# A recurrence, a gated convolution and an FFT mixer on one core: the recurrence in 64-token halves and plain fp32

## The chip, the cores and the metric

The kernel runs on one core of a Trainium2 chip. TensorE multiplies matrices into PSUM (eight banks), VectorE, ScalarE and GpSimd work on tiles, and DMA queues move data; GpSimd works in SBUF alone. The metric is the time on the device in microseconds (us). One profiled execution was traced.

## The reference

Four batches, 768 tokens, eight heads of 40, width 320. Cut to what is computed:

```python
for t in range(S):                       # a recurrence with a state C of 40x40 and n of 40 per head
    m_new = np.maximum(f_gate[:, :, t] + m, i_gate[:, :, t])
    f_stab = np.exp(f_gate[:, :, t] + m - m_new)
    i_stab = np.exp(i_gate[:, :, t] - m_new)
    C = f_stab * C + i_stab * outer(vt, kt)
    n = f_stab * n + i_stab * kt
    y[:, :, t] = sigmoid(o_gate[:, :, t]) * (C @ qt) / np.maximum(np.abs(n @ qt), 1.0)
x = y.transpose(0, 2, 1, 3).reshape(B, S, 320)
gate = sigmoid(sum(conv_w[k] * xp[:, k:k + S, :] for k in range(5)))    # causal, by channel
x = (gate * (x @ w_val)) @ w_out
mixed = np.real(np.fft.fft(np.fft.fft(x, axis=1), axis=2))
u = x + mixed
un = (u - mean(u)) / np.sqrt(var(u) + 1e-06)
out = u + np.maximum(un @ w_ch1, 0.0) @ w_ch2                           # 320 -> 1280 -> 320
```

## The kernel before

Every operation is first recorded into a plan (`_Plan.add`, units of one engine each) and then issued in the order of a list, `ORDER`, written out for all engines at once; `CELL` names the buffer of each tile and `FILLS` says ahead of which unit how many filler matmuls (`fill`, L1099, tile `void`, 128 x 128 in fp32) go into TensorE's queue. All operations but the fillers carry line L332 in the profile, so they are told apart by their tiles.

A batch is worked in this order. The recurrence takes six chunks of 128 tokens (`loads`, `a_pre`, `a_s`, `a_p`, `a_u`, `a_pv`, `a_fin`, `a_tr`). The gates' decay is first made for all tokens (`prologue_gates`); per chunk, VectorE scans it into a 128 x 128 triangle per head (`d`, two scans of 512), from rows that a DMA spreads over 128 partitions (`scr`). Scores `s` are keys by queries: in batch 0 in plain fp32, with the heads of a pair in the lower and the upper 64 partitions; from batch 1 on in fp32r, for which q and k are split into a high and a low part (`a_split`, tile `HL`) and twelve DMAs a chunk set three copies one below the other (`qk3`, 120 rows). VectorE multiplies scores and decay. `u` is the chunk's update of the state (`kvo` by `kvo`, 40 columns), added into `cc` on GpSimd and VectorE and copied into a block-diagonal `cbd`; `pv` is the output from the state (`e` by `cbd`) and from the scores (`d` by `kvo`). `a_fin` divides and gates, `a_tr` transposes (`tp`) into halves of 384 tokens.

Per half, `p_conv` adds five shifted products (one on ScalarE, four on VectorE, tile `gate`), `p_val`, `p_g` and `p_z` multiply with `w_val` and `w_out` in fp32r, each operand split into high and low. `p_fold` (GpSimd) and `b_s`, `b_se`, `d_mm`, `b_d`, `b_de` do the two Fourier transforms by matmuls with cosine and sine tables (`ap`, `uv`), the tables and operands split as well. `b_ln` and `b_ut` normalise and transpose, and the MLP runs per 256 tokens in ten tiles of 128 hidden columns: `m_1` (`hp`, eight matmuls), ScalarE and VectorE split its relu into `hh` and `hl`, `m_2` adds six matmuls into two `acc`. Weights arrive as 64-bit numbers and are turned into fp32 on the chip (`to_f32`, tile `mk`, mostly VectorE). While one batch's MLP runs, the list works the next batch's recurrence in between.

Of the kernel before, what the change touches and what calls it, by code (L numbers as in the profile page):

```python
# [1236 lines left out]
```

## Time and profile before

| what | us |
|---|---|
| median of three runs (lowest, highest) | 582.0 (581.72, 584.56) |
| the profiled execution, its span | 583.1 |
| TensorE busy in it | 559.4 |
| VectorE busy | 428.3 |
| ScalarE, GpSimd busy | 250.8, 250.3 |

The span runs from the first to the last instruction of the profiled execution; the profile shows no time around it. A matmul counts as busy from its start to its modelled end, and fillers count as any matmul does, so TensorE's share says how full its queue is and not how much of the work is the kernel's own.

### The profile page before, as it was taken

Reading aid. Unit: us, or ns where it says so; the run is one execution under the profiler, and the core shown is the slowest. Engines: PE = TensorE matmul, PEld = TensorE weight load, DVE = VectorE, ACT = ScalarE, POOL = GpSimd, SP = SyncE. Lnnn points to the kernel's source line nnn. Section 1 sums busy time; section 2 is a strip of 40 time slices with the busy share of each in tenths; the row PEclk is TensorE's granted clock in tenths of the full one; section 3 lists DMA queues with packets and bytes.
Section 4 is the critical chain, followed back from the end, with each engine's and each line's share of the span. In section 5 each row is a group of like instructions: output and inputs, shape, how many; then the busy total and the mean of one; then the engine's idle time right before and its main releaser. Section 6 shows DMA issues by size and latency. Waiting matters only on the chain.

```text
span 583.1 us, 12342 instructions
## 1 busy us (share of the span) xinstructions
PE 559.4 (96%) x4564; PEld 542.7 (93%) x4564; DVE 428.3 (73%) x904; ACT 250.8 (43%) x635; POOL 250.3 (43%) x301
## 2 busy tenths in 40 slices
PE   9999999999999979899999999999999999999997
PEld 8999899989999869899899898899999999999997
DVE  6737989989788999976689867945997375484322
ACT  3322343443365444535355534454445353444221
POOL 5246567649656434547632313365441315220000
PEclk9999999999999987999899999999999999999999
DMA  9997453635546849445422756426541200000000
GB/s 289 273 248 188 145 125 99 174 113 163 177 148 185 258 143 239 147 146 163 139 70 73 219 177 197 103 69 194 148 143 50 76 2 22 1 2 24 24 24 22
DMA packets 90843, 75.83 MB, mean 130 GB/s; under 512 B 5536, under 2 KB 83488, under 8 KB 90784
## 3 DMA queue, kind: packets, MB, share of 16 engines
q1 hardware_dynamic: 90032, 72.80, 43.2%
q0 software_dynamic: 752, 2.25, 1.3%
q8 instruction: 36, 0.59, 0.4%
q14 instruction: 23, 0.19, 0.1%
HBM read 53.21 MB, written 4.13 MB: 98 GB/s over the span
## 4 chain that ended last, share of the span: by engine, by line
PE 59%; DVE 15%; DMA 12%; issue 5%; SPq 4%; ACT 2%; POOL 2%; DVEq 0%; POOLq 0%; ACTq 0%
PE acc L332 14%; PE hp L332 13%; PE void L1099 7%; PE pv L332 7%; DVE d L332 6%; PE ap L332 5%; SPq L332 4%; PE val L332 4%; PE zp L332 3%; DMA kvo<-in_kvo_dram 3%; PE tp L332 2%; DMA qk<-HL 2%; DMA raw<-in_w_dram 2%; DMA d<-scr 2%; DVE mk L332 2%
## 5 line engine op out<-in xcount | busy, mean ns | idle before, releaser
L1099 PE MATMUL void<-ones 128*128 128x128 f32 x866 | 106.6, 282 | 1.0 <-DVE mhalf L332 1.0
L1099 PEld LDWEIGHTS void<-ones 128*128 128x128 f32 x866 | 102.4, 197 | 1.7 <-DVE mhalf L332 1.0
L332 PE MATMUL hp<-uu,w1H 128*128 128x256 f32 x480 | 93.6, 287 | 2.7 <-DVE hl L332 1.3
L332 DVE SCALAR_TENSOR_TENSOR hl<-hp,hh 128x256 fp32r<-128x256 f32 x120 | 48.9, 415 | 46.0 <-ACT hh L332 44.5
L332 PEld LDWEIGHTS hp<-uu,w1H 128*128 128x128 f32 x480 | 75.9, 191 | 4.4 <-DVE hl L332 1.9
L332 PE MATMUL acc<-w2H,hl 128*128 128x320 f32 x240 | 77.0, 321 | 2.3 <-DVE hl L332 2.2
L332 PE MATMUL acc<-w2H,hh 128*128 128x320 f32 x240 | 78.2, 326 | 0.5 <-ACT hh L332 0.5
L332 ACT ACTIVATE hh<-hp 128x256 fp32r<-128x256 f32 x120 | 45.3, 379 | 72.9 <-PE acc L332 48.0
L332 PE MATMUL acc<-w2L,hh 128*128 128x320 f32 x240 | 75.5, 315 | 0.0
L332 DVE TENSOR_TENSOR_SCAN d<-d,ipat 128x512 f32<-128x512 f32 x44 | 67.5, 1563 | 1.9 <-DMA d<-scr 1.8
L332 PE MATMUL hp<-uu,w1L 128*128 128x256 f32 x240 | 67.8, 283 | 0.0
L332 DVE SCALAR_TENSOR_TENSOR gate<-xT,cw,gate 128x384 f32<-128x384 f32 x96 | 63.9, 693 | 5.1 <-ACT gate L332 4.9
L332 PE MATMUL pv<-kvo,d 128*128 128x41 f32 x384 | 54.4, 275 | 1.5 <-DVE d L332 1.3
L332 PEld LDWEIGHTS pv<-kvo,d 128*128 128x128 f32 x384 | 50.2, 193 | 2.3 <-DVE d L332 1.9
L332 PEld LDWEIGHTS acc<-w2H,hl 128*128 128x128 f32 x240 | 46.3, 193 | 5.1 <-DVE hl L332 4.6
L332 PEld LDWEIGHTS acc<-w2H,hh 128*128 128x128 f32 x240 | 46.4, 193 | 1.1 <-ACT hh L332 0.8
L332 PEld LDWEIGHTS acc<-w2L,hh 128*128 128x128 f32 x240 | 46.3, 193 | 0.0
L332 PEld LDWEIGHTS hp<-uu,w1L 128*128 128x128 f32 x240 | 45.9, 191 | 0.0
L332 POOL TENSOR_TENSOR kvo<-kvo,r 128x320 f32<-128x320 f32 x24 | 20.2, 843 | 50.6 <-DVE r L332 48.5
L332 POOL TENSOR_TENSOR e<-e,qk 128x512 f32<-128x512 f32 x20 | 27.6, 1383 | 26.1 <-issue 12.4
L332 DVE TENSOR_TENSOR d<-s,d 128x512 f32<-128x512 f32 x48 | 32.3, 679 | 6.2 <-POOL kvo L332 4.4
L332 PE MATMUL hp<-uu,w1T 128*128 128x256 f32 x120 | 33.9, 282 | 0.0
(171 smaller groups left out, 1260.9 us busy)
## 6 DMA issues: line engine op xcount, KB each, us to landing
qk<-HL SPq DMA_DIRECT2D x216, 80.0 KB
qk<-in_qk_dram SPq DMA_DIRECT2D x24, 512.0 KB
kvo<-in_kvo_dram SPq DMA_DIRECT2D x24, 484.0 KB
d<-scr SPq DMA_DIRECT2D x22, 512.0 KB
raw<-in_w_dram SPq DMA_DIRECT2D x9, 640.0 KB
e<-sce SPq DMA_DIRECT2D x40, 128.0 KB
out_dram<-z SPq DMA_DIRECT2D x24, 160.0 KB
cs<-in_c_cs_dram POOLq DMA_DIRECT2D x2, 776.0 KB, 6.2
```

What stands on the lines that cost most here:

```text
L332: getattr(engine, method)(*a, **k)
L1099: nc.tensor.matmul(out=void[0], lhsT=ones.real(), rhs=ones.real(), start=True, stop=True)
```

## The change

The recurrence works each chunk in two halves of 64 tokens: the decay triangles are 64 x 64 (`d` is 8 heads x 64, one scan), the scores, the update and the outputs are matmuls in plain fp32 on 64 partitions to 64 columns, and the state is carried twice a chunk (`cc` of three tiles; no `cbd`). The halves of odd heads are swapped on the host side. The split of q and k and its copies (`a_split`) are gone. The decay rows reach PSUM by a matmul with a selector (`a_fb`, `sel`, `gsp`) and no longer by DMA, and the scan reads them there. The convolution accumulates in PSUM, and five of its 24 pieces, all of batch 0, are matmuls with diagonal matrices (`diagonals`). The Fourier tables and operands are no longer split. The MLP's tiles are worked in pairs of 128 hidden columns. Some steps change engine (`XL`, `ES` to VectorE, the small steps of the norm, `N_`, to GpSimd), weight tails of 64 rows are converted two at a time and copied to the other 64 partitions by DMA, PSUM is one tile of eight banks that the list `CELL` hands out, `ORDER` is another list of 2,002 units (2,795 before), and the fillers named in `FILLS` are 75 (433 before).

```diff
+LS = 64
-BF = 1
-CF = 6
-LAG = 1
+NQK = 2
+PECONV = [(0, 0, 0), (0, 0, 1), (0, 0, 2), (0, 1, 0), (0, 1, 2)]
...
+FILLS = [
+    (137, 11, 5), (60, 2, 2), (64, 4, 6), (142, 6, 5), (165, 3, 6), (170, 4, 2), (226, 6, 6), (390, 1, 1), (396, 7,
+    4), (401, 2, 2), (435, 2, 1), (459, 4, 1), (464, 2, 1), (488, 13, 6), (518, 8, 6),
+]
...
+                if k.pop("drain", False):
+                    engine.drain()
...
+    def fill(n, k):
+        a = pat.real()[:, 0:L]
+        for _ in range(n):
+            nc.tensor.matmul(out=banks()[:, k, 0:L], lhsT=a, rhs=a, start=True, stop=True)
...
+    def prologue_spread():
+        fh = wt("fh", [32, S], "M", F32R)
+        fl = wt("fl", [32, S], "M", F32R)
+        A.activation(fh, f0, AF.Copy)
+        V.tensor_tensor(fl, f0, f(fh), op=ALU.subtract)
+        for n, x in enumerate((fh, fl)):
+            SP.dma_start(out=scr[n, :, 0:32:2].rearrange("g r t -> r g t"), in_=hs(f(x[0:32:2])))
+            for h in range(2):
+                SP.dma_start(out=scr[n, 1 - h:NG:2, 1:32:2].rearrange("g r t -> r g t"), in_=hs(f(x[1:32:2]))[:, h:NG:2])
+        for b in range(1, B):
+            SP.dma_start(out=f(gsp[32 * b - 32:32 * b - 8]),
+                         in_=scr[:, :, b * H:b * H + H].rearrange("n g h t -> (n g) (h t)"))
...
+            A.activation(his[n][r], m[r], AF.Copy)
+            G.tensor_tensor(los[n][r], m[r], f(his[n][r]), op=ALU.subtract)
+            SP.dma_start(out=f(his[n][o]), in_=f(his[n][r]))
+            SP.dma_start(out=f(los[n][o]), in_=f(los[n][r]))
...
+    def a_fb(b, c):
+        fb = mm("fb", [128, H, LS])
+        if b == 0:
+            for h in range(H):
+                for x in range(2):
+                    g = 2 * c + (x ^ (h % 2))
+                    T.matmul(out=fb[64 * x:64 * x + 64, h, :], lhsT=ident[0:32, h:h + 1].to_broadcast([32, LS]),
+                             rhs=f0[:, LS * g:LS * g + LS], start=True, stop=True)
         else:
+            r = slice(32 * b - 32, 32 * b - 8)
+            g = gsp[r].rearrange("r (h t) -> r h t", h=H)
+            T.matmul(out=fb, lhsT=sel[r, L * c:L * c + L], rhs=g, start=True, stop=True)
+        fbs[b, c] = fb
...
+        fb = fbs.pop((b, c))
+        d = wt("d", [128, H, LS], "B")
+        V.tensor_tensor_scan(d.rearrange("p h t -> p (h t)"), fb.rearrange("p h t -> p (h t)"), ipat, 0.0,
+                             op0=ALU.mult, op1=ALU.add)
+        t["d"] = d
...
-        e = wt("HL", [128, 4, 2, L], HLB, F32R)
-        A.activation(e[:, 1:3], x, AF.Copy)
-        V.tensor_tensor(e[:, 0:4:3], x, f(e[:, 1:3]), op=ALU.subtract)
-        s3 = wt("qk3", [3 * D, 2, 2, 2 * L], QKB, F32R)
-        for n, m in enumerate((slice(1, 3), slice(0, 3, 2), slice(1, 4, 2))):
-            for s in range(2):
-                SP.dma_start(out=f(s3[n * D:n * D + D, :, s]), in_=f(e[64 * s:64 * s + D, m]).rearrange("r a p t -> r a (p t)"))
...
+    def a_s(b, c):
         t = ld[b, c]
+        sp = mm("s", [128, 2, 4, LS], 2)
+        for p in range(4):
+            for x in range(2):
+                for s in range(2):
+                    r = slice(64 * s, 64 * s + D)
+                    m = slice(LS * (x ^ s), LS * (x ^ s) + LS)
+                    T.matmul(out=sp[64 * x:64 * x + 64, s, p, :], lhsT=t["k"][r, p, m], rhs=t["q"][r, p, m],
+                             start=True, stop=True, skip_group_check=True)
...
+        n = 1 if c == NC - 1 else 2
+        u = mm("u", [128, n, 4, E], n)
+        for p in range(4):
+            for x in range(n):
+                for s in range(2):
+                    r = slice(64 * (x ^ s), 64 * (x ^ s) + 64)
+                    h = 2 * p + s
+                    T.matmul(out=u[64 * s:64 * s + 64, x, p, :], lhsT=t["kvo"][r, D * h:D * h + LS], rhs=t["vp"][r, h],
+                             start=True, stop=True, skip_group_check=True)
+        t["cc"] = []
+        for x in range(n):
+            g = 2 * c + x
+            cc = ccs[g % 3]
+            if g > 0:
+                G.tensor_tensor(cc, st_c["C"],
+                                fcol[:, 4 * b:4 * b + 4, g].unsqueeze(2).to_broadcast([128, 4, E]), op=ALU.mult)
+                V.tensor_tensor(cc, cc, u[:, x], op=ALU.add)
...
+        pv = mm("pv", [128, 2, 4, E], 2)
+        first = set()
+
+        def go(lhsT, rhs, x, s, p, last):
+            k = (x, s) not in first
+            first.add((x, s))
+            T.matmul(out=pv[64 * x:64 * x + 64, s, p, :], lhsT=lhsT, rhs=rhs, start=k, stop=last and p == 3,
+                     skip_group_check=True, **({"drain": True} if (last, x, s, p) == (True, 0, 0, 0) else {}))
+
+        plan.join = True
         for p in range(4):
+            for x in range(c == 0, 2):
+                for s in range(2):
+                    r = slice(64 * s, 64 * s + D)
+                    go(t["e"][r, p, LS * x:LS * x + LS], t["cc"][x][r, p], x, s, p, False)
+        n = b * NC + c + 2
+        if n < B * NC:
+            a_fb(*divmod(n, NC))
+        else:
+            T.transpose(mm("void", [128, L]), ident, ident)
+        for p in range(4):
+            for x in range(2):
+                for s in range(2):
+                    r = slice(64 * (x ^ s), 64 * (x ^ s) + 64)
+                    h = 2 * p + s
+                    go(t["d"][r, h], t["vp"][r, h], x, s, p, True)
+        plan.join = False
         t["pv"] = pv
...
+    def diagonals():
+        for j in range(3):
+            dg[j] = wt("dg", [128, 5, 128], "M")
+            G.tensor_tensor(dg[j], ident.unsqueeze(1).to_broadcast([128, 5, 128]),
+                            cw[:, j].unsqueeze(2).to_broadcast([128, 5, 128]), op=ALU.mult)
+
+    def p_conv(b, hf, j):
         xT = xs[b, hf][0]
+        if j == 0:
+            gs[b, hf] = {"gH": wt("gH", [128, 3, HALF], "A", F32R), "gL": wt("gL", [128, 2, HALF], "M", F32R)}
+        a = mm("cv", [128, HALF])
+        if (b, hf, j) in PECONV:
+            for k in range(5):
+                T.matmul(out=a, lhsT=dg[j][:, k], rhs=xT[:, j, k:k + HALF], start=k == 0, stop=k == 4)
+        else:
+            A.activation(a, xT[:, j, 0:HALF], AF.Copy, scale=cw[:, j, 0:1])
+            for k in range(1, 5):
+                V.scalar_tensor_tensor(
+                    out=a, in0=xT[:, j, k:k + HALF], scalar=cw[:, j, k:k + 1], in1=a,
+                    op0=ALU.mult, op1=ALU.add,
+                )
...
+            for n in range(2):
+                for t in {"c": [0], "s": [1], "t": [0, 1]}[which]:
+                    j = 2 * (a ^ t) + n
+                    m = {"c": slice(0, 128), "s": slice(192, 320), "t": slice(128, 192)}[which]
+                    ops.append((t, eot[b, (j + 1) // 2][:, m], cs[t][:, j]))
             if a == 0 and which != "s":
-                m = slice(0, 128) if which == "c" else slice(128, 256)
-                xh, xl = eot[b, "x"]
-                ops += [(xh[:, m], exr), (xl[:, m], exr)]
-            for n, (l, r) in enumerate(ops):
-                T.matmul(out=ap_[:, a], lhsT=l, rhs=r, start=n == 0, stop=n == len(ops) - 1)
+                m = slice(0, 128) if which == "c" else slice(128, 192)
+                ops.append((0, ex[:, m], exr))
+            for n, (t, l, r) in enumerate(ops):
+                same = [k for k, o in enumerate(ops) if o[0] == t]
+                o = ap_[64 * t:64 * t + 64, a, 0:NQ] if which == "t" else ap_[:, a, 0:NQ]
+                T.matmul(out=o, lhsT=l, rhs=r, start=n == same[0], stop=n == same[-1])
...
+        ops = [(at[b, "CS"[t]][:, m], dmat[:, t, 0]), (at[b, "T"][:, m], dmat[:, t, 1])]
...
+        hp = mm("hp", [128, 2, 256])
+        for q in range(2):
+            m = slice(256 * n + 128 * q, 256 * n + 128 * q + 128)
+            ops = []
+            for k in range(2):
+                ops += [(w1H[:, k, m], uH[:, k]), (w1H[:, k, m], uL[:, k]), (w1L[:, k, m], uH[:, k])]
+            ops += [(w1T[:, m], uH[:, 2]), (w1U[:, m], uH[:, 2])]
+            for x, (l, r) in enumerate(ops):
+                T.matmul(out=hp[:, q], lhsT=l, rhs=r, start=x == 0, stop=x == len(ops) - 1)
+        hh = wt("hh", [128, 2, 256], "B", F32R)
+        hl = wt("hl", [128, 2, 256], "B", F32R)
...
+    XL, ES, N_ = V, V, G
```

## Rows read from the trace of the kernel before

**Rows 1.** Page, busy time of each engine: us, share of the span, instructions.

```profile
PE 559.4 (96%) x4564; PEld 542.7 (93%) x4564; DVE 428.3 (73%) x904; ACT 250.8 (43%) x635; POOL 250.3 (43%) x301
```

**Rows 2.** Table by stage, cut where the first `hp` starts: PE, PEld, DVE, ACT, POOL.

```profile
0.00:179.20 179.20, 175.21 (x1589) 170.29 (x1589) 144.67 (x245) 71.73 (x168) 104.26 (x120) 1.00 0.63 178
179.20:583.20 404.00, 384.19 (x2978) 372.45 (x2977) 283.58 (x660) 179.02 (x467) 146.04 (x182) 0.98 0.37 109
```

**Rows 3.** The same table for the filler matmuls (`void`) alone.

```profile
0.00:179.20 179.20, 106.38 (x866) 1.00 0.63 178
```

**Rows 4.** Chain of waits, in order of time: start, us, what, records.

```profile
119.31 5.41 PE void L1099 x48
...
226.14 2.60 PE pv L332 x24
...
296.13 2.43 PE uv L332 x20
...
301.78 2.80 PE val L332 x16
...
457.69 1.01 PE tp L332 x9
...
488.84 3.54 PE zp L332 x24
...
497.49 1.76 PE acc L332 x12
...
499.25 2.81 PE hp L332 x24
...
502.06 6.47 PE ap L332 x52
```

**Rows 5.** TensorE in order of time, a chunk of batch 0: start, us, form, records.

```profile
59.77 0.69 PE L332 MATMUL u<-kvo 128*40 128x41 f32 x16 [0.83 <-DVE d L332]
...
60.42 0.42 PE L332 MATMUL pv<-cbd,e 128*128 128x82 f32 x2
...
66.55 1.16 PE L332 MATMUL s<-qk 64*128 64x128 f32 x16
...
67.64 0.45 PE L332 MATMUL pv<-cbd,e 128*128 128x82 f32 x2
```

**Rows 6.** TensorE in order of time: batch 0's last `tp`, the first `hp`.

```profile
108.43 0.49 PE L332 MATMUL tp<-ipat,x 128*128 128x128 f32 x3
...
179.18 0.73 PE L332 MATMUL hp<-uu,w1H 128*128 128x256 f32 x2
```

**Rows 7.** Table by stage around the stretches at half clock; PEclk is third from the end.

```profile
210.00:215.40 5.40, 2.20 (x17) 1.79 (x15) 5.31 (x11) 1.72 (x4) 0.53 (x1) 1.00 0.25 80
...
215.40:225.70 10.30, 9.52 (x41) 9.33 (x42) 9.78 (x21) 2.29 (x6) 4.82 (x6) 0.50 0.59 174
...
246.20:249.60 3.40, 3.40 (x16) 3.40 (x15) 3.34 (x6) 0.09 (x1) 0.00 (x0) 0.50 0.32 99
```

**Rows 8.** VectorE's groups: form, count, busy us, mean ns, idle before.

```profile
L332 DVE TENSOR_TENSOR_SCAN d<-d,ipat 128x512 f32<-128x512 f32 x44 | 67.5, 1563 | 1.9 <-DMA d<-scr 1.8
...
L332 DVE SCALAR_TENSOR_TENSOR gate<-xT,cw,gate 128x384 f32<-128x384 f32 x96 | 63.9, 693 | 5.1 <-ACT gate L332 4.9
...
L332 DVE TENSOR_TENSOR d<-s,d 128x512 f32<-128x512 f32 x48 | 32.3, 679 | 6.2 <-POOL kvo L332 4.4 <-PE s L332 1.6
...
L332 DVE TENSOR_TENSOR HL<-qk,HL 128x512 fp32r<-128x512 f32 x36 | 29.3, 817 | 3.8 <-ACT HL L332 3.6 <-issue 0.2
...
L332 DVE TENSOR_TENSOR_SCAN d<-fb,ipat 128x512 f32<-128x512 f32 x4 | 4.7, 1206 | 1.2 <-PE fb L332 1.2
```

**Rows 9.** GpSimd's groups, columns as before.

```profile
L332 POOL TENSOR_TENSOR e<-e,qk 128x512 f32<-128x512 f32 x20 | 27.6, 1383 | 26.1 <-issue 12.4 <-PE pv L332 6.7 <-DMA e<-sce 6.1
...
L332 POOL TENSOR_TENSOR kvo<-kvo,r 128x320 f32<-128x320 f32 x24 | 20.2, 843 | 50.6 <-DVE r L332 48.5 <-DVE t L332 2.1
...
L332 POOL TENSOR_TENSOR cc<-cc,fcol 104x164 f32<-104x164 f32 x16 | 12.2, 764 | 11.0 <-DVE cc L332 5.5 <-ACT cc L332 2.7 <-ACT r L332 1.8
```

More of the change, by code (lines that the diff above doesn't have):

```diff
@@ L309, in add @@
         if u is None or eng.name != "T" or u.engine != "T" or u.rank != self.rank or not (
-                u.out is out or u.out.name == out.name == "s"):
-            u = _Unit(self.rank, eng.name, out)
+                self.join or u.out is out):
+            u = _Unit(self.rank, eng.name, out, self.what)
             self.units.append(u)
@@ L318, in add @@
                 x.t.n = len(self.tiles)
-            u.tiles.add(x.t)
     def emit(self):
-        held = [t for t in self.tiles if t.tag is not None]
+        held = [t for t in self.tiles if t.kind is not None]
         for t, n in zip(held, CELL, strict=True):
-            t.tag, t.bufs = "slot%d" % n, 1
-        fills = dict(FILLS)
+            t.cell = n
+        fills = {n: (m, k) for n, m, k in FILLS}
         for n in ORDER:
-            for _ in range(fills.get(n, 0)):
-                self.fill()
+            if n in fills:
+                self.fill(*fills[n])
             for engine, method, a, k in self.units[n].calls:
@@ L390, in mixer_kernel, with banks, wt @@
-    dmat = ct("dmat", [128, 2, 2, NL], F32R)
-    dtail = ct("dtail", [128, 2, NL], F32R)
-    exr = ct("exr", [1, NK], F32R)
+    dr_ = ctx.enter_context(tc.tile_pool(name="dr", bufs=1, space=DRAM))
+    bank = []
+    def banks():
+        if not bank:
+            bank.append(ps_.tile([128, 8, 512], F32, name="bank"))
+        return bank[0]
+    def ct(name, shape, dt=F32):
+        return _Tile(cst_, shape, dt, name, None)
+    def wt(name, shape, kind, dt=F32):
+        return _Tile(wk_, shape, dt, name, kind)
@@ new lines, in mm @@
+    def mm(name, shape, banks_=1, kind="ps"):
+        return _Tile(banks, shape, F32, name, kind, banks_)
+    def fill(n, k):
+        a = pat.real()[:, 0:L]
+        for _ in range(n):
+            nc.tensor.matmul(out=banks()[:, k, 0:L], lhsT=a, rhs=a, start=True, stop=True)
+    plan.fill = fill
+    pat = ct("pat", [128, L + 512])
+    ident, ipat = pat[:, 0:L], pat[:, L:]
+    sel = ct("sel", [96, S], F32R)
+    gsp = ct("gsp", [96, H * LS], F32R)
+    cs = [ct("cs%d" % t, [128, 4, NQ]) for t in range(2)]
@@ L608, in a_pre @@
         iv = isT[:, c, b * H:(b + 1) * H]
-        G.tensor_tensor(t["vp"], t["vp"], iv.unsqueeze(2).to_broadcast([128, H, D + 1]), op=ALU.mult)
-        if not (b == 0 and c < 2):
-            for g in range(2):
-                d = t["d"][:, 4 * g:4 * g + 4].rearrange("p h t -> p (h t)")
-                V.tensor_tensor_scan(d, d, ipat, 0.0, op0=ALU.mult, op1=ALU.add)
-        if c < NC - 1:
-            G.tensor_tensor(t["kd"], t["kd"], t["d"][:, :, L - 1].unsqueeze(2).to_broadcast([128, H, D]), op=ALU.mult)
@@ L686, in a_pv @@
     def a_pv(b, c):
         t = ld[b, c]
-        pv = ps.tile([128, H, D + 1], F32, name="pv", tag="att", bufs=2)
-        for p in range(4):
-            if c > 0:
-                T.matmul(out=pv[:, 2 * p:2 * p + 2, :], lhsT=t["e"][:, p, :],
-                         rhs=cbd[(c - 1) % 2][:, 2 * p:2 * p + 2, :], start=True, stop=False)
-            for s in range(2):
-                h = 2 * p + s
-                T.matmul(out=pv[:, h, :], lhsT=t["d"][:, h, :], rhs=t["vp"][:, h, :], start=c == 0, stop=c == 0 or s == 1)
+        pv = mm("pv", [128, 2, 4, E], 2)
@@ L905, in b_d @@
         if i == 0:
-            x1 = ps.tile([1, NL], F32, name="x1", tag="tr", bufs=1)
+            x1 = mm("x1", [1, NL])
             d_mm(b, x1, 0, slice(HALF, HALF + 1))
@@ L953, in b_ln @@
             un[b, i, hf] = u
-        un[b, i] = (lambda t: (t[:, 0:3], t[:, 3:5]))(wt("uu", [128, 5, 256], 2, F32R))
+        un[b, i] = (lambda t: (t[:, 0:3], t[:, 3:5]))(wt("uu", [128, 5, 256], "UU", F32R))
     def b_ut(b, i, hf):
         u = un.pop((b, i, hf))
-        tp = ps.tile([128, 3, L], F32, name="tp", tag="tr", bufs=1)
-        for j in range(3):
-            T.transpose(tp[:, j, :], u[:, 128 * j:128 * j + 128], ident)
+        tp = mm("tp", [128, 3, L])
+        tr3(tp, u)
         uH, uL = un[b, i]
@@ L987, in m_2 @@
         if n == 0:
-            ml[b, i] = [ps.tile([128, DM], F32, name="acc", tag="acc", bufs=2) for _ in range(2)]
+            ml[b, i] = [mm("acc", [128, DM], 1, "acc") for _ in range(2)]
         for hf in range(2):
+            acc = ml[b, i][hf]
             m = slice(hf * L, hf * L + L)
-            acc = ml[b, i][hf]
-            T.matmul(out=acc, lhsT=hh[:, m], rhs=w2H[:, n], start=n == 0, stop=False)
-            T.matmul(out=acc, lhsT=hh[:, m], rhs=w2L[:, n], start=False, stop=False)
-            T.matmul(out=acc, lhsT=hl[:, m], rhs=w2H[:, n], start=False, stop=n == 9)
+            for q in range(2):
+                T.matmul(out=acc, lhsT=hh[:, q, m], rhs=w2H[:, 2 * n + q], start=n + q == 0, stop=False)
+                T.matmul(out=acc, lhsT=hh[:, q, m], rhs=w2L[:, 2 * n + q], start=False, stop=False)
+            for q in range(2):
+                T.matmul(out=acc, lhsT=hl[:, q, m], rhs=w2H[:, 2 * n + q], start=False, stop=n == 4 and q == 1)
     def m_out(b, i):
@@ L1090, in run @@
-    def run(fn):
-        plan.rank += 1
-        fn()
-    void = []
-    def fill():
-        if not void:
-            void.append(ps_.tile([128, L], F32, name="void", tag="slot7", bufs=1))
-        nc.tensor.matmul(out=void[0], lhsT=ones.real(), rhs=ones.real(), start=True, stop=True)
-    plan.fill = fill
-    run(prologue_gates)
-    run(prologue_const)
-    run(lambda: loads(0, 0))
-    run(lambda: loads(0, 1))
-    craw = {}
-    run(lambda: craw.update(t=conv_weights()))
-    run(lambda: V.tensor_copy(cw.rearrange("p j k -> p (j k)"),
-                              to_f32(craw["t"], 3, 5).rearrange("p j k -> p (j k)")))
@@ L1111, in mixer_kernel, with run @@
-    for load, go in wpieces:
-        run(load)
-        run(go)
-    run(prologue_cs)
-    for b in range(B):
-        for fn in a_pieces(b) + f_pieces(b) + u_pieces(b, 0) + u_pieces(b, 1) + u_pieces(b, 2):
-            run(fn)
+    XL, ES, N_ = V, V, G
+    def run(what, fn, *a):
+        plan.rank += 1
+        plan.what = (what,) + a
+        fn(*a)
+    run("pads", prologue_pads)
+    run("gates", prologue_gates)
+    run("const", prologue_const)
+    for b in range(B):
+        for c in range(NC):
+            run("loads", loads, b, c)
+            if (b, c) == (0, 3):
+                run("spread", prologue_spread)
+            if (b, c) == (0, 1):
+                run("cw", conv_weights)
+                run("dg", diagonals)
+                run("wvo", weights_vo)
+            if (b, c) == (0, 5):
+                for n in range(5):
+                    run("wff", weights_ff, n)
+            if b == 0 and c < 2:
+                run("fb", a_fb, b, c)
+            run("pre", a_pre, b, c)
+            run("s", a_s, b, c)
+            run("u", a_u, b, c)
+            run("pv", a_pv, b, c)
+            run("fin", a_fin, b, c)
+            run("tr", a_tr, b, c)
+            if c % 3 == 2:
+                hf = c // 3
+                for j in range(3):
+                    run("conv", p_conv, b, hf, j)
+                    run("val", p_val, b, hf, j)
+                    run("g", p_g, b, hf, j)
+                for i in range(3):
+                    run("z", p_z, b, hf, i)
+        for w in "cts":
+            run("fft", b_s, b, w)
+            run("ffte", b_se, b, w)
+        for i in range(3):
+            run("d", b_d, b, i)
+            run("de", b_de, b, i)
+            run("ln", b_ln, b, i)
+            for hf in range(2):
+                run("ut", b_ut, b, i, hf)
+        for i in range(3):
+            for n in range(5):
+                run("m1", m_1, b, i, n)
+                run("m2", m_2, b, i, n)
+            run("out", m_out, b, i)
```

732 lines of the change are left out of this document (259 added, 473 removed), and 303 rows, old and new, of tables (CELL, ORDER).

## The prediction, written before the change was run

> **What bounds the kernel now.** I read the busy shares of the page first. TensorE is busy for 559.4 of 583.1 us and VectorE for 428.3 [rows 1], which looks like a kernel with no room on TensorE. The table by stage, cut where the first MLP matmul starts, shows that this is two kernels. The first `hp` matmul starts at 179.18 us [rows 6]. Ahead of it TensorE is busy for 175.2 of 179.2 us, but the same table for the `void` matmuls alone gives 106.4 us of that [rows 2, 3]: they are fillers written into the queue, so real work is 175.2 - 106.4 = 68.8 us. In that stretch VectorE works 144.7 us, 81% [rows 2]: batch 0 is held by VectorE and by loads, and TensorE waits on them. All 866 filler records lie there. Behind 179.2 us TensorE is busy 384.2 of 404.0 us and VectorE 283.6 [rows 2]: there TensorE sets the end.
>
> So the time is T1 (when the first MLP matmul starts) plus TensorE's work behind it, plus what is lost there. For prices I take the chain of waits where a kind of matmul runs alone [rows 4]. 48 filler records take 5.41 us, 0.113 us each; a plain fp32 matmul leaves two records (866 for the 433 fillers that the list asks for), so 128 columns cost 0.225 us. A unit of eight `hp` matmuls takes 2.81 / 3 = 0.94 us, six `acc` 0.88, eight `val` 1.40, eight `zp` 3.54 / 3 = 1.18, a batch's `ap` 6.47, and 20 `uv` records 2.43.
>
> Check of these prices on the kernel before, behind 179.2 us: MLP 120 x (0.94 + 0.88) = 218; 18 `val` 25; 18 `zp` 21; 38 groups of three transposes at 1.01 / 3 = 0.34 [rows 4] 13; three `ap` 19; three `uv` of 35 records 13; 16 chunks of the recurrence at 4.4 (24 `pv` records 2.60 [rows 4], `u` 0.65 [rows 5], eight `s` records and the changeovers about 1.15, an estimate from the same rows) 70. Sum 379, and 384 are busy. The 25 us between sum and 404 are: 8.5 for half of the 17 us that ran at clock 0.50 (one stretch of 10.3 us and two of 3.4, of which one stands in [rows 7]), some 4 of tail, and 12 of gaps.
>
> **The change, part by part.**
>
> *The recurrence on TensorE.* Each chunk of 128 tokens now runs as two halves of 64, in matmuls of 64 x 64 or 40 x 64, all plain fp32: `s` 16, `u` 16, `pv` 16 from the state and 16 from the scores, 64 matmuls or 128 records, plus one `fb` selector matmul of 512 columns (0.22 us by width, from the `hp` price). What a record costs hangs on whether the four quadrants of the array run at once. Batch 0's old `s` has two row halves in alternation: 16 records of full width from 66.55 to the next kind at 67.64 us, 1.09 us [rows 5]. One at a time they would cost 16 x 0.113 = 1.80; two at a time 0.90, and 0.19 is left for the changeover. So row halves overlap. `u` fills its two column halves one after the other: 16 records 40 columns wide would be 16 x 0.113 x 40 / 128 = 0.56, and 0.65 is taken, so its changeover is 0.09 and it says nothing of column halves. A 64-column record is therefore 0.056 us alone, 0.028 in pairs, 0.014 in fours. I take 0.018, nearer to fours: the new loops name the four quadrants in turn, and in `s` the second half added nothing that I can see. Then 128 x 0.018 = 2.3; eight changeovers at 0.12 (bounds 0.09 and 0.19) 1.0; the drain ahead of the last part of `pv`, which no row shows, 0.1 (from 0 to two changeovers, 0.4). With `fb` 3.6 us a chunk, bounds 1.8 + 0.2 + 0.7 = 2.7 and 3.6 + 0.2 + 1.5 + 0.4 = 5.7, against 4.4 before.
>
> The Trainium skill says in TensorEngine Tiling (Array Packing), Performance Considerations, Instruction Overhead, that each matmul has about 60 cycles of overhead, so that tiling must not be taken from a dimension that is small already. At 2.4 GHz that is an estimate of 25 ns a record and 3.2 us in place of 2.3 for the chunk. No row here shows such a floor, since the narrowest records, 40 columns, go by at 0.65 / 16 = 0.041.
>
> *Constants and operands in plain fp32.* `ap` falls from 52 fp32r records to 18 matmuls of 193 columns a batch, two records each: 2 x 193 x 0.113 / 128 = 0.34 us a matmul. The eight of the `t` part alternate between column halves: 1.4 at once, 2.7 if not; I take 1.4. Sum (9 + 1) x 0.34 + 1.4 = 4.8 (to 6.1) for 6.47. `uv` falls from 35 records to 12 matmuls of 161 columns and a small pair: 12 x 0.28 + 0.2 = 3.6 for 4.3. Convolution on TensorE: five of the 24 pieces, all of batch 0, five matmuls of 384 columns, 5 x 0.68 = 3.4 each, 17 us, ahead of T1. Fillers fall from 433 to 75, all ahead of T1. MLP, `val` and `zp` keep their matmuls: 0.
>
> *VectorE.* The scans of the decay fall from 48 to 24, and out of PSUM they cost 1.206 and not 1.563 us: 72 to 29 us. Products with the scores fall from 48 x 0.679 to 24. The 19 convolutions that stay work with one operand in PSUM; an add of 512 elements with one costs 0.679 where 384 elements in SBUF cost 0.693 [rows 8], so about 0.55 (0.52 to 0.69): 11 us less, and 14 for the five that move. The `HL` split (36 x 0.817) is gone. Second parts of splits that go (`eh`, `AH`, the extra row) are worth 22 us, the layer norm's steps that leave 13, the paired `hl` 8. Against it `es`, `os`, `xL`, the tails and two folds move over from GpSimd, 100-odd operations at 0.3 to 0.55, about 44 us, and the state's second half adds 4. In all 428 - 43 - 16 - 25 - 29 - 22 - 13 - 8 + 44 + 4 = 320, and ahead of T1, counted over the new list, 95 us for 144.7. Behind T1 this is under TensorE's work: 0; it would cost only if VectorE went back over 95%. MLP tiles in pairs: one `hl` of 512 for two of 256, also under TensorE. The layer norm's small steps go to GpSimd, seven at 0.3 for 0.2 or less on VectorE; on the path once, in batch 0, 1.5 us.
>
> *Loads and the SP queue.* 216 `HL` copies and the 22 spreads of the decay over 128 partitions leave the queue, 386 DMA issues become 198, so no load waits behind them; that goes into T1. Against it twelve small copies of weight tails now stand on SP, each waiting for ScalarE or GpSimd; queued behind the first four are the decay rows `e` of chunk 5 and the next weight piece. While loads run two chunks ahead that costs 0; if not, a chunk comes some 6 us late, and T1's upper bound holds it. The drain stands in TensorE's own queue, so its 0.1 us is paid by all that follows.
>
> *T1.* GpSimd is the next limit in batch 0: six chunks with three 0.84 us products, one 1.38 and two `cc` at 0.76 [rows 9], 5.4 us each, plus three diagonals and weight pieces, about 46 us from about 14 us on: 60 at the earliest, 70 at 80% busy, until the last chunk's transpose, which before came at 108.43 [rows 6]. From there to the first `hp` took 70.8 us; now the chain (convolution 6.8, `val` 4.2, gates 3, `zp` 3.5, fold 3, `ap` 4.8, its folding 1.4, `uv` 3.6, adds 2.7, layer norm 4.6, transposes and splits 4.5) makes 42, and some 30 handovers and the weight pieces between make it 52. T1 = 122; VectorE's 95 us at its old 81% give 117. Bounds 60 + 46 = 106 and 84 + 66 = 150.
>
> *Sum.* Behind T1: 218 + 25 + 21 + 13 + 3 x 4.8 + 3 x 3.6 + 17.7 chunks x 3.6 (64) = 366. Lost: gaps 12, tail 4, clock 3 (guessed at a third of before). 122 + 366 + 19 = **507 us**. It is made against the profiled span of 583.1, which is 1.1 above the median of 582.0, so the two need no correction.
>
> **The rivals.**
> *Records bound by their issue or only in pairs* (0.028): 5.0 us a chunk, 1.4 x 23.7 = 33 more: 540. For it: only pairs are shown [rows 5]. Against: the loops are written for fours. The skill's 60 cycles, named above, would come to much the same.
> *The clock falls in batch 0.* After a stretch with TensorE busy for 2.2 of 5.4 us the granted clock was 0.50 for 10.3 us [rows 7], and 358 fillers go. On the path to T1 lie about 36 us of matmuls; at half clock throughout 36 more: 543. Against: real work ahead of T1 is as much as before in two thirds of the time. The Trainium skill has the same in TensorE: Matmul & The Clock Gate, HAM oscillation: idle gaps between bursts of matmuls send the clock back to half. The trace agrees with its 0.50.
> *Everything overlaps*: four at once and T1 = 106: 106 + 350 + 15 = 471.
> *Slower:* quadrants don't overlap at all. Then 128 x 0.056 = 7.2, 8.5 us a chunk, 4.9 x 23.7 = 116 more: 623. It decides from 0.043 us a record on, where the chunk costs 6.8. Against it stands the old `s`; only a clash of the halves over a PSUM bank could bring it.
> *Nothing changes*: new waits of the one list eat all of it; no row speaks for that.
>
> **How the numbers follow.** 507 within 480 to 530: 0.53. Pairs or issue: 0.13. Clock: 0.14. All overlaps: 0.11. Slower: 0.06. No change, within 0.5% (about what a measurement of this kernel can tell from none): 0.03. The range of 465 to 555 leaves out the slower case, no change and parts of the clock's and the best case, under 2 in 10. Faster 0.91, same 0.03, slower 0.06.
>
> **What would show it.** The first `hp` near 122 us; 32 `s` records in about 0.6 us; `pv` near 1.4; an `ap` batch near 4.8; TensorE over 95% busy behind the first `hp`, and granted clock 1.0 there. I am wrong if T1 stays over 150, if 32 small records take over 1 us, or if TensorE idles behind T1 on a bank or on GpSimd.

## The result and the profile after

The change made the kernel faster: 511.65 us median (511.07 to 512.76) against 581.86 (578.95 to 584.56) in the same comparison, ratio 0.8795, 95% interval 0.8756 to 0.8835. I forecast 507 within 465 to 555. The profiled span is 509.3 us; the device time of the same execution is 511.18, 1.9 above it. The forecast was added up from the span of the kernel before, so 507 stands against 509.3.

In the kernel after, all PSUM is one tile `bank`, all operations carry L290 and fillers L340, so kinds of matmul are told apart by their inputs: `uu,w1H` is `hp`, `w2H,hh` is `acc`, `xH,wvH` is `val`, `pat,x` is `tp`, `kvo` is `u`, `qk` is `s`, `f,pat` is batch 0's `fb`, `xT,dg` the convolution's pieces, `kvo,d` and `cc,e` are the two parts of `pv`. First the page's busy times, then the table by stage, cut at the first `hp` (they answer to [rows 1, 2]), then TensorE in order of time (to [rows 6]):

```profile
PE 471.6 (93%) x5826; PEld 429.0 (84%) x5826; DVE 319.9 (63%) x740; ACT 176.7 (35%) x389; POOL 182.0 (36%) x299
```

```profile
0.00:124.40 124.40, 100.30 (x1389) 84.18 (x1390) 87.09 (x197) 48.84 (x103) 65.86 (x95) 0.95 0.52 152
124.40:509.30 384.90, 371.27 (x4439) 344.80 (x4437) 232.81 (x543) 127.81 (x287) 116.15 (x205) 0.99 0.18 55
```

```profile
28.17 1.97 PE L290 MATMUL bank<-f,pat 32*64 32x64 f32 x32
...
34.48 1.15 PE L290 MATMUL bank<-f,pat 32*64 32x64 f32 x32
...
51.35 9.95 PE L290 MATMUL bank<-xT,dg 128*128 128x384 f32 x30
61.23 0.69 PE L290 MATMUL bank<-qk 40*64 40x64 f32 x32
62.59 0.45 PE L290 MATMUL bank<-xH,wvH 128*128 128x384 f32 x1 [0.67 <-ACT gate L290]
...
66.99 0.69 PE L290 MATMUL bank<-qk 40*64 40x64 f32 x32
...
82.06 0.52 PE L290 MATMUL bank<-pat,x 128*128 128x128 f32 x3 [0.23 <-DVE x L290]
...
124.44 0.48 PE L290 MATMUL bank<-uu,w1H 128*128 128x256 f32 x2
...
139.01 0.55 PE L290 MATMUL bank<-pat,x 128*128 128x128 f32 x3
...
148.08 0.68 PE L290 MATMUL bank<-kvo,d 64*64 64x41 f32 x32
148.68 0.41 PE L290 MATMUL bank<-w2H,hh 128*128 128x320 f32 x1
...
149.75 0.69 PE L290 MATMUL bank<-qk 40*64 40x64 f32 x32
150.37 0.50 PE L290 MATMUL bank<-uu,w1H 128*128 128x256 f32 x2
```

T1, the start of the first `hp`, came from 179.18 to 124.44 us; the stretch behind it went from 404.0 to 384.9 us. So of 73.8 us of span, 54.7 lie ahead of T1 and 19.1 behind. Ahead of it VectorE works 87.1 us for 144.7; behind it TensorE is busy 371.3 for 384.2 and VectorE 232.8 for 283.6. The 32 `s` records take 0.62 us from their start to the next kind (149.75 to 150.37), the 32 of `pv` 0.60 (148.08 to 148.68). At 128 columns a record costs 0.113 [rows 4], so 64 columns alone would be 0.056, 32 of them 1.8 us, and in pairs 0.9: more than two run at once. In the trace the 32 `s` records start in fours, 6 or 7 ns apart within a four and 58 or 59 ns from one four to the next (the first four took longer), so it is four quadrants at once.

### The profile page after: what moved, and what is told of

Its sections match the earlier page's. It is cut to its first block, busy times and chain, and to the rows that moved or that the text cites. A ratio compares the mean times of both kernels' runs of the same rounds, so it can differ in the third digit from the quotient of the medians.

```text
span 509.3 us, 14016 instructions
## 1 busy us (share of the span) xinstructions
PE 471.6 (93%) x5826; PEld 429.0 (84%) x5826; DVE 319.9 (63%) x740; ACT 176.7 (35%) x389; POOL 182.0 (36%) x299
## 4 chain that ended last, share of the span: by engine, by line
PE 60%; DVE 18%; issue 6%; POOL 5%; ACT 4%; DMA 2%; SPq 1%; POOLq 0%; ACTq 0%; DVEq 0%
PE bank L290 59%; DVE bank L290 6%; DVE mk L290 4%; DVE z L290 2%; POOL r L290 2%; PE bank L340 1%; DMA raw<-in_w_dram 1%; SPq L290 1%; POOL t L290 1%; DVE gg L290 1%; DVE bs L290 1%; DVE d L290 1%; DVE hl L290 1%; POOL nb L290 1%; DMA kvo<-in_kvo_dram 1%
## 5 line engine op out<-in xcount | busy, mean ns | idle before, releaser
L290 PE MATMUL bank<-uu,w1H 128*128 128x256 f32 x480 | 93.1, 287 | 0.4 <-DVE gg L290 0.2
L290 PE MATMUL bank<-w2H,hh 128*128 128x320 f32 x240 | 76.4, 326 | 0.1
L290 PEld LDWEIGHTS bank<-uu,w1H 128*128 128x128 f32 x480 | 74.0, 189 | 2.0 <-issue 0.6
L290 PE MATMUL bank<-w2L,hh 128*128 128x320 f32 x240 | 72.6, 310 | 0.0
L290 DVE SCALAR_TENSOR_TENSOR hl<-bank,hh 128x512 fp32r<-128x512 f32 x60 | 41.1, 688 | 47.5 <-ACT hh L290 46.4
L290 ACT ACTIVATE hh<-bank 128x512 fp32r<-128x512 f32 x60 | 35.6, 596 | 93.2 <-PE bank L290 89.4
L290 PE MATMUL bank<-uu,w1L 128*128 128x256 f32 x240 | 67.2, 280 | 0.0
L290 PE MATMUL bank<-w2H,hl 128*128 128x320 f32 x240 | 55.3, 312 | 0.5 <-DVE hl L290 0.5
L290 PEld LDWEIGHTS bank<-w2H,hh 128*128 128x128 f32 x240 | 45.6, 190 | 1.3 <-DVE z L290 0.2
L290 PEld LDWEIGHTS bank<-w2L,hh 128*128 128x128 f32 x240 | 45.7, 191 | 0.0
L290 DVE SCALAR_TENSOR_TENSOR bank<-xT,cw,bank 128x384 f32<-128x384 f32 x76 | 45.2, 617 | 0.7
L290 PEld LDWEIGHTS bank<-uu,w1L 128*128 128x128 f32 x240 | 45.4, 189 | 0.0
L290 PEld LDWEIGHTS bank<-w2H,hl 128*128 128x128 f32 x240 | 40.2, 189 | 1.4 <-DVE hl L290 1.4
L290 DVE TENSOR_TENSOR_SCAN d<-bank,pat 128x512 f32<-128x512 f32 x24 | 29.2, 1216 | 11.4 <-PE bank L290 11.3
L290 PE MATMUL bank<-uu,w1T 128*128 128x256 f32 x120 | 33.6, 280 | 0.0
L290 PE MATMUL bank<-uu,w1U 128*128 128x256 f32 x120 | 33.6, 280 | 0.0
L290 POOL TENSOR_TENSOR kvo<-kvo,r 128x320 f32<-128x320 f32 x24 | 17.9, 746 | 42.2 <-DVE r L290 41.5
L290 POOL TENSOR_TENSOR cc<-cc,fcol 128x164 f32<-128x164 f32 x40 | 18.8, 469 | 38.0 <-PE bank L290 17.1
L290 POOL TENSOR_TENSOR gL<-gg,gH 128x384 fp32r<-128x384 f32 x16 | 16.2, 1016 | 41.0 <-ACT gH L290 41.0
L290 POOL TENSOR_TENSOR e<-e,qk 128x512 f32<-128x512 f32 (+1 forms) x24 | 28.4, 1188 | 6.5 <-DMA qk<-in_qk_dram 4.3
L290 DVE TENSOR_TENSOR z<-z,bank 128x159 f32<-128x159 f32 (+2 forms) x72 | 24.9, 369 | 8.5 <-PE bank L290 8.2
L290 POOL TENSOR_TENSOR kvo<-kvo,d 128x320 f32<-128x320 f32 x24 | 18.5, 770 | 32.6 <-DVE d L290 19.0
```

The source lines that it names most:

```text
L290: getattr(engine, method)(*a, **k)
```

## The experiments

All times are medians beside runs of the kernel before on the same chip; T1 is from each run's one profile. a_ve_more, the last run below, changes nothing ahead of T1 and still had it 1.9 us later than the kernel after, so a difference of T1 of some 2 us shows nothing. "a" kernels are edits of the kernel after, "b" kernels of the kernel before.

**What set T1 in the kernel before.** I had said VectorE and loads. First its convolution adds of batch 0 went:

```diff
+            if b == 0:
+                plan.units.append(_Unit(plan.rank, "V", None))
+                continue
             V.scalar_tensor_tensor(
                 out=g, in0=xT[:, j, k:k + HALF], scalar=cw[:, j, k:k + 1], in1=g,
```

> The kernel before with the 24 convolution adds of batch 0 on VectorE left out (part of the computation is left out). They are 24 of about 0.8 us, 19 us of VectorE's 144.7 ahead of the first hp matmul. If VectorE's work sets that point, as I argued, it comes 12 to 19 us earlier and the whole run takes 563 to 570 us. If loads or GpSimd's products set it, the point moves by less than 4 us and the run stays above 577.

580.35 us, ratio 0.9947 (0.991 to 0.9985), T1 177.76. The table by stage, cut at T1:

```profile
0.00:177.70 177.70, 174.57 (x1587) 170.09 (x1588) 127.35 (x221) 71.45 (x168) 99.61 (x120) 1.00 0.62 179
```

VectorE lost 17 us of its 144.7 and T1 moved by 1.4, which is within the scatter. My account of batch 0 fell here, with one way out: TensorE's queue, fillers included, was still busy 174.6 of 177.7 us, and a queue padded to the full can't go faster than its padding. So half of the later fillers went too, alone and with the adds; from the entry of unit 354 on every count is halved (of the list, its first changed entries):

```diff
-FILLS = [(18, 21), ... (344, 8), (354, 20), (374, 6), (380, 2), (399, 32), ...]
+FILLS = [(18, 21), ... (344, 8), (354, 10), (374, 3), (380, 1), (399, 16), ...]
```

> The kernel before with half of the 257 fillers behind its 60th microsecond left out (131 fillers, 29.6 us of TensorE). VectorE's work is as it was. If VectorE sets the first hp matmul, it stays near 179 us and the run within 578 to 590 (the upper end if the clock falls). If the fillers fill TensorE's queue so tightly that they set it, the first hp comes 10 us or more earlier and the run is under 573.

> The same half of the fillers left out, and the 24 convolution adds of batch 0 too (part of the computation is left out). With the fillers alone unchanged the adds moved the first hp by 1.4 us only, since TensorE's queue, fillers included, was full. If VectorE sets batch 0 behind that padding, the first hp now comes at 162 to 168 us and the run takes 563 to 571. If it stays over 175 us with the run near b_half, VectorE's work is not what sets it and loads or GpSimd do.

b_half: 584.12 us, 1.0052 (1.0015 to 1.0088), T1 179.09. b_conv_half: 579.87, 0.9946 (0.991 to 0.9982), T1 176.65. Neither the padding nor the adds behind the padding moved T1 by much more than the scatter. The test has a flaw: with fewer fillers the granted clock ahead of T1 fell from 1.00 to 0.93 and 0.92, and what that cost may hide a gain. In the chain of waits of b_conv_half stood something that I had counted only as being in the way of loads ("no load waits behind them"):

```profile
105.96 0.66 PE s L332 x3
...
107.52 0.80 SPq L332
...
108.37 0.77 SPq L332
...
109.18 0.77 SPq L332
...
110.81 5.76 DMA qk<-HL
...
116.81 0.65 PE s L332 x4
```

SP issues the copies of the split q and k one by one, 0.8 us each, for scores of batch 1 that the old list puts ahead of T1. So two of three copies went, alone and with the adds, the fillers still halved:

```diff
                 SP.dma_start(out=f(s3[n * D:n * D + D, :, s]), in_=f(e[64 * s:64 * s + D, m]).rearrange("r a p t -> r a (p t)"))
+                if n > 0:
+                    plan.units[-1].calls = []
...
-                T.matmul(out=sp[:, 2 * s + p, :], lhsT=s3[:, 1, s, r], rhs=s3[:, 0, s, r], start=True, stop=True)
+                T.matmul(out=sp[:, 2 * s + p, :], lhsT=s3[0:D, 1, s, r], rhs=s3[0:D, 0, s, r], start=True, stop=True)
```

> The kernel before with half of the fillers behind its 60th microsecond (as in b_half: first hp 179.1 us, 584 us) and with two of three copies of the split q and k left out, 144 of 216 (the scores then lack the products of their low parts). In the chain of waits of the run with fewer adds and fillers, four rows of 0.8 us copies on SP and their landings stand between 107 and 142 us, for scores of batch 1 that the list puts ahead of the first hp. If these copies set that stretch, the first hp comes 8 to 20 us earlier, at 159 to 171, and the run takes 560 to 576. If VectorE's work or the loads set it, it stays over 175 us and the run over 578.

> The same, with the 24 convolution adds of batch 0 left out as well (part of the computation is left out). If the copies alone set the stretch ahead of the first hp, it comes within 3 us of the run with the adds. If copies and VectorE's work lie close behind one another, so that neither shows alone, it comes at 150 to 162 us and the run takes 550 to 567.

b_copies: 581.81 us, 0.997 (0.9938 to 1.0003), T1 178.95. b_conv_copies: 576.03, 0.9887 (0.9824 to 0.995), T1 170.37. So with the fillers halved the adds were worth 2.4 us of T1 while the copies stood, and 8.6 without them; the copies 0.1 while the adds stood, and 6.3 without. The chains of waits fit two waits close behind one another: in b_copies, with the copies gone, the adds (`gate`) stand where the copies stood:

```profile
109.71 6.77 DVE gate L332 x7
...
116.86 1.13 DVE gate L332 x2
```

Two things weaken this reading. The clock wasn't the same: the tables by stage ahead of T1, of b_half, b_conv_half, b_copies and b_conv_copies, give 0.93, 0.92, 0.93 and 0.97 (third from the end), so part of the 8.7 us from the first to the last may be clock. And the whole time shows hardly any of the joint effect: by medians the adds are worth 4.3 us with the copies and 5.8 without, since behind T1 b_conv_copies takes 404.1 us where b_copies takes 399.2.

```profile
0.00:179.10 179.10, 159.43 (x1327) 151.56 (x1327) 142.85 (x246) 71.79 (x168) 102.79 (x121) 0.93 0.63 178
...
0.00:176.60 176.60, 160.24 (x1325) 152.69 (x1326) 125.83 (x220) 71.80 (x168) 98.83 (x120) 0.92 0.65 180
...
0.00:178.90 178.90, 161.00 (x1325) 152.36 (x1326) 145.69 (x244) 71.84 (x168) 101.78 (x120) 0.93 0.59 164
...
0.00:170.40 170.40, 154.92 (x1327) 146.68 (x1327) 127.38 (x220) 71.65 (x168) 101.02 (x120) 0.97 0.61 172
```

Even so it is 8.7 us of the 54.7, and T1 stayed above the 150 to 162 that I expected. In the chain of waits of b_conv_copies the next links stand in place: GpSimd's work on `es` and `os`, which the change moves to VectorE, and the `HL` split, which it drops:

```profile
122.97 0.68 POOL os L332
123.82 1.46 POOL es L332
125.28 1.74 POOL os L332
127.02 1.65 POOL eo L332 x2
...
129.67 0.92 POOL es L332
...
131.87 1.22 DVE HL L332
```

**What sets T1 in the kernel after.** The five convolution pieces on TensorE went back to ScalarE and VectorE, at the same places of the list (`attach` keeps a piece's adds in one unit):

```diff
         if (b, hf, j) in PECONV:
-            for k in range(5):
-                T.matmul(out=a, lhsT=dg[j][:, k], rhs=xT[:, j, k:k + HALF], start=k == 0, stop=k == 4)
+            A.activation(a, xT[:, j, 0:HALF], AF.Copy, scale=cw[:, j, 0:1])
+            plan.attach = True
+            for k in range(1, 5):
+                V.scalar_tensor_tensor(
+                    out=a, in0=xT[:, j, k:k + HALF], scalar=cw[:, j, k:k + 1], in1=a,
+                    op0=ALU.mult, op1=ALU.add,
+                )
+            plan.attach = False
```

> The changed kernel with its five TensorE convolution pieces back on ScalarE and VectorE. VectorE gains 20 adds of 0.62 us, 12.4 us, ahead of the first hp matmul; TensorE loses 17 us there. If VectorE (and the chain through it) sets that point, it moves from 124.4 to 130 to 137 us and the run takes 517 to 524. If loads or GpSimd set it: within 2 us of 511.7. If TensorE's own queue set it: up to 10 us faster.

530.8 us, 0.9106 (0.9076 to 0.9135), T1 142.05. The table by stage, and TensorE in order of time where the first three pieces stood:

```profile
0.00:142.00 142.00, 92.37 (x1340) 83.17 (x1341) 99.02 (x217) 51.19 (x108) 65.76 (x95) 0.82 0.46 133
142.00:528.30 386.30, 372.27 (x4438) 345.96 (x4436) 232.81 (x543) 127.85 (x287) 115.97 (x205) 0.99 0.18 54
```

```profile
50.09 0.68 PE L293 MATMUL bank<-kvo,d 64*64 64x41 f32 x32
59.42 1.25 PE L293 MATMUL bank<-qk 40*64 40x64 f32 x32 [8.65 <-ACT wvU L293]
68.21 0.69 PE L293 MATMUL bank<-xH,wvH 128*128 128x384 f32 x1 [7.54 <-ACT gate L293]
...
74.99 0.69 PE L293 MATMUL bank<-qk 40*64 40x64 f32 x32
```

VectorE has 11.9 us more, T1 is 17.6 later (142.05, where I expected 130 to 137), and the stretch behind it is much the same (386.3 for 384.9). TensorE stands empty for the pieces and the granted clock ahead of T1 is 0.82 for 0.95, so lost clock is part of it. At least 3.6 us can be read: the 24 `val` matmuls of the first half take 6.78 us (68.21 to 74.99) for the 4.40 of the kernel after (62.59 to 66.99), the last eight of the second half 2.72 for 1.51, and both stand in the chain of waits. The next kernel kept the matmuls and computed the pieces behind them as well:

```diff
                 T.matmul(out=a, lhsT=dg[j][:, k], rhs=xT[:, j, k:k + HALF], start=k == 0, stop=k == 4)
+            plan.attach = True
+            A.activation(a, xT[:, j, 0:HALF], AF.Copy, scale=cw[:, j, 0:1])
...
```

> The changed kernel whose five TensorE convolution pieces keep their matmuls and are computed on ScalarE and VectorE after them as well (the matmuls' results are overwritten). TensorE keeps its work, VectorE has 12.4 us more, as in the run with the pieces on VectorE alone (first hp at 142.05 us, 530.8 us). If VectorE's added work made that 19 us, the first hp stays at 138 to 144 and the run at 526 to 533. If most of it was the lost clock (TensorE empty for 11 to 17 us at a time), the first hp comes at 129 to 136 and the run takes 516 to 524.

538.62 us, 0.9241 (0.9192 to 0.929), T1 152.35: later still, outside both expectations. The edit wasn't clean: ScalarE's first step now waits for the matmuls, and in the chain of waits a piece's matmuls, that step and the four adds stand one behind another:

```profile
59.31 5.16 PE bank L293 x10
...
64.53 0.59 ACT bank L293
...
65.15 0.63 DVE bank L293
...
67.12 0.62 DVE bank L293
```

T1 moved by 27.9, 5.6 a piece. ScalarE's step and four adds of 0.617 are 3.1 of that; waiting for a piece's matmuls (9.95 for three, 3.3 each, in the kernel after) can be the rest. The clock ahead of T1 is 0.90, so this run doesn't separate the clock from the adds either. What the two runs show is that work put into VectorE's queue at these places delays T1 by more than its own time, though VectorE is busy only 87 of 124 us in the kernel after.

**Fillers and the clock.** `FILLS = []` in either kernel; and the kernel after with 12 more fillers in gaps:

```diff
+    (58, 5, 4), (228, 4, 0), (183, 2, 0), (199, 1, 2),
```

> The changed kernel with none of its 75 fillers. If the clock ahead of the first hp hangs on real work, 511 to 516. If 75 fillers at the right places hold it, more stretches at granted clock 0.50 ahead of the first hp and over 520 us. If they cost time, under 510.

> The kernel before with none of its 433 filler matmuls (866 records, 106 us of TensorE). If they only cover time in which TensorE waits, and keep its clock, the run stays at 578 to 592: nothing to gain, and a longer time by what the granted clock falls ahead of the first hp. If they held real work back, so that 358 fewer of them explain part of the gain of the change, it falls under 575.

> The changed kernel with 12 more fillers in four gaps of TensorE ahead of its half-clock stretches (13.7 us of them ahead of the first hp). If idle gaps bring the clock down, some of these stretches go and the run gains up to 6 us: 505 to 510. If the gaps aren't the cause, or the fillers hold real work back, 511 to 515.

a_nofill: 519.79 us, 0.8924 (0.8879 to 0.8969), T1 133.17. b_nofill: 598.56, 1.027 (1.0227 to 1.0312), above the 592 that I expected at most, T1 193.55, granted clock 0.63 ahead of it. a_fillgaps: 510.47, 0.8746 (0.868 to 0.8811), T1 124.68. So 75 fillers are worth 8 us and 433 were worth 16; no run shows them to cost anything, and 358 fewer of them explain no gain. Twelve more halve the time at clock 0.50 ahead of T1 (6.8 for 13.7 us), T1 stays, and the interval overlaps that of the kernel after: no difference shown. It stays open, for two of the four executions, at 505.63 and 508.02, lie below all four of the kernel after.

**Quadrants, and what sets the end behind T1.** In a_pairs the loops of `s`, `u` and `pv` name the column half outermost, so that only row halves alternate. Of `s`:

```diff
-        for p in range(4):
-            for x in range(2):
+        for x in range(2):
+            for p in range(4):
                 for s in range(2):
```

> The changed kernel with the loops of the recurrence in another order, so that consecutive matmuls differ in their row half alone and the column half changes once. By my theory two run at once and not four: 0.028 in place of 0.015 us a record, 128 records a chunk, 1.8 us a chunk, 24 chunks; since TensorE sets the end behind the first hp (17.7 chunks), 30 to 40 us slower, 541 to 552. If the column half costs nothing to change and the array takes four from further back in the queue: within 3 us of 511.7. If TensorE didn't set the end: the 32 s records take 1 us or more, and the run stays under 520.

525.01 us, 0.9003 (0.8932 to 0.9073), T1 126.97. TensorE in order of time, then the table by stage:

```profile
151.89 0.93 PE L290 MATMUL bank<-kvo,d 64*64 64x41 f32 x32
152.75 0.42 PE L290 MATMUL bank<-w2H,hh 128*128 128x320 f32 x1
...
153.82 0.97 PE L290 MATMUL bank<-qk 40*64 40x64 f32 x32
154.73 0.51 PE L290 MATMUL bank<-uu,w1H 128*128 128x256 f32 x2
```

```profile
127.00:524.90 397.90, 387.00 (x4438) 361.04 (x4436) 233.20 (x543) 127.62 (x287) 116.06 (x205) 1.00 0.17 53
```

32 `s` records take 0.91 us for 0.62, `pv` 0.86 for 0.60: two at a time, and in the trace most starts now come in twos. Behind T1 TensorE is busy 15.7 us more and the stretch is 13.0 longer. The loss is less than half of what I expected because pairs cost 0.22 us a kind on average (15.7 us over 17.7 chunks of four kinds) and not 0.45; of what they do cost, five sixths reach the end.

In a_ve_more VectorE got a multiply behind each `hl`:

```diff
         V.scalar_tensor_tensor(out=hl, in0=hp, scalar=0.0, in1=f(hh), op0=ALU.max, op1=ALU.subtract)
+        plan.attach = True
+        V.tensor_tensor(junk, ipat, ipat, op=ALU.mult)
+        plan.attach = False
```

> The changed kernel with a VectorE multiply of 512 elements (about 0.65 us, result unused) put right behind each of the 60 hl operations of the MLP: 39 us more on VectorE, all behind the first hp, where it is busy 233 of 385 us. If TensorE alone sets that stretch: 511 to 518. If VectorE's queue stands on the path there as it did ahead of the first hp (12.4 us more cost 17.6): 535 to 555.

530.86 us, 0.9101 (0.9043 to 0.916), T1 126.38. Between the two expectations. The group added, and the table by stage:

```profile
L293 DVE TENSOR_TENSOR junk<-pat 128x512 f32<-128x512 f32 x60 | 45.5, 758 | 0.0
```

```profile
126.40:530.80 404.40, 377.27 (x4439) 347.35 (x4436) 271.89 (x603) 128.20 (x287) 120.60 (x205) 0.99 0.17 52
```

The 45.5 us of multiplies make VectorE 39.1 us busier (some of it overlaps), from 60% to 67% of the stretch, and the stretch 19.5 us longer, though TensorE is busy only 6 us more; the rest is TensorE waiting. The multiply isn't simply in the way of the `acc` matmuls behind `hl`: TensorE's waits for `hl` grow only from 0.8 to 2.9 us, and the others are for other work of VectorE and ScalarE. So TensorE doesn't set that stretch alone.

## Why the prediction was right, step by step

*The cut at the first `hp`* held: 122 + 385 forecast, 124.4 + 384.9 measured. Both parts came out through errors that cancel, so a match this close is luck, though the mechanism of the gain on TensorE was right.

*T1.* Right in sum, wrong in its working. The last `tp` of batch 0, forecast at 70 from GpSimd's rate at 80% busy, came at 82.06, and GpSimd was busy for 36.5 of the 63.9 us from 14.0 to 77.9, 57% and not the 80% that the term rests on. The chain from there to the first `hp`, forecast at 52, took 42.4. The cross-check, VectorE's 95 us at 81%, has no standing: VectorE works 87 of 124 us, 70%, and b_conv_out shows that its busy share didn't set the old T1. The sentence that "batch 0 is held by VectorE and by loads" read a busy share as a bound. What the runs show in its place: in the old kernel the chain of waits shifts with each edit, from SP's copies to VectorE's adds to GpSimd's `es` and `os`; two links together took 8.7 us, some of which may be clock, and 2.4 and 0.1 alone. In the new kernel work put into VectorE's queue at the convolution's places moves T1 by more than its own time. Of the 54.7 us, 26.4 lie ahead of batch 0's last `tp` (108.43 to 82.06, [rows 6]) and 28.4 behind it. In the latter the old list also puts three chunks of batch 1 ahead of T1 (their `tp` at 143.19, 161.01 and 178.71 us in TensorE's order of time), the new one none (its first at 139.01). That shift, the loads and the scans weren't tried one by one: how the other 46 us divide between them stays open.

*The convolution on TensorE* was costed at 17 us of TensorE and 14 of VectorE; a_conv_ve shows it to be worth 17.6 us of T1 with the list as it is, a quarter of the whole gain and the largest single part that a run isolates; at least 3.6 of it came by the clock. The prediction didn't price it by itself.

*Behind T1.* I counted time from the first record of each kind to the next kind's first, summed over the trace: recurrence 52 us for the 64 forecast, `hp` and `acc` 232.6 for 218, `val` and `zp` 48.6 for 46, `tp` 12.1 for 13, `ap` 14.3 for 14.4, `uv` 12.0 for 10.8; 372 for 366. Lost on top were 13.6 us (384.9 less the 371.3 that TensorE is busy) for the 19 forecast. The MLP was mis-sized: my prices from rows of the chain left out what a unit loses at its changeover (the old kernel gives 232.9 the same way). The recurrence erred the other way: 0.60 to 0.62 us a kind of 32 records with its changeover, where I took 32 x 0.018 + 2 x 0.12 = 0.82. The prediction's check on the old kernel, 379 for 384, had passed by the same two errors: MLP 218 for 232.9, and recurrence 70 for 59.2 by this count, since the records behind T1 are those of 14.3 chunks (344 of `pv`, 24 a chunk) and not of 16.

*The quadrants* run in fours, as taken; a_pairs shows the rival's case and that it wasn't this one: pairs cost 13 us, where 33 were forecast. The Trainium skill's rule (TensorEngine Tiling (Array Packing), Performance Considerations, Instruction Overhead: some 60 cycles a matmul) I had applied to each record, 25 ns by estimate; 32 records in 0.60 us, 19 ns with the changeover, speak against that. A matmul here leaves two records, and per matmul the 37 ns of the row don't contradict it.

*VectorE behind T1 at 0* is the step that failed: it "would cost only if VectorE went back over 95%", and a_ve_more shows it to cost at 67%, 0.4 us for each us of the multiplies and 0.5 for each us that VectorE is busier. The change took 50.8 us off VectorE in that stretch; TensorE's busy time fell by 12.9 while the stretch fell by 19.1, so some 6 us came out of TensorE's waits. a_ve_more makes it likely that part of these is VectorE's relief, but it adds work and takes none off; the split wasn't measured.

*The clock*: it was 0.95 ahead of T1, so the rival with half clock throughout didn't come, but fillers do hold part of it: the run takes 8 us more without them.

## What to carry to other kernels

A queue that is 98% busy with fillers hides who sets the pace, and a busy share of 81% on another engine doesn't name it either: follow the chain of waits in the stretch. When one suspect removed shows nothing, remove two together, and read the granted clock and the whole time beside the stretch, for an edit that thins TensorE's queue moves the clock too. Work in the queue that a chain runs through can cost more than its own time (17.6 us of T1 for 11.9 of VectorE's, at least 3.6 of them by the clock). An engine at 60% beside a TensorE that is 96% busy isn't free: ask what a microsecond more on it costs.
